# Bigbird attention into a gated MLP: two heads' block rows by one SBUF DMA, and two output steps of batch 0 in one slot

## The chip, the cores and the metric

One core of a Trainium2 chip runs the whole program. The metric is the device time of one execution in microseconds (us); the time before is the median of three runs.

## What is computed

Block-sparse attention over 4 batches, 8 heads, 768 positions and head size 64, followed by a gated MLP over the joined heads:

```
mask = window of +-1 block | first and last block (rows and columns) | 3 sampled blocks per row   # blocks of 32
attn = softmax(where(mask, q k^T / 8, -1e9)) ;  x = attn v            # heads joined: [4, 768, 512]
h = relu(x @ w_in) ; u, v = halves of h
v_n = (v - mean) / sqrt(var + 1e-6)
out = (u * (w_spatial @ v_n + b_spatial)) @ w_out                      # [4, 768, 512] float32
```

## The kernel before

**The mask inside the product.** The tile `kq` has 88 partitions: 64 hold the head size, and 24 (`MR`, partitions 64 to 87) hold *block rows*. For a key column a block row says which of the 24 blocks the key lies in (one-hot); for a query column it says which blocks the query's block may see (0 or -300). One matmul over 88 rows then gives masked scores. For every head `kq` holds 768 key columns (`K_`) and 768 query columns, the queries in three thirds of 256 (`qcols(t)`). The block rows are the same for all heads. They are computed once, for head 0: the keys' by `one_hot` on VectorE, the queries' by three small matmuls (`mask_rows`), which ScalarE (`m0`, `m1`) and VectorE (`m2`) copy into `kq`. Then they are copied to the other heads: `rows` (line 248) copies them on VectorE, and one DMA (line 328) writes the second and third query thirds of heads 2 to 7.

**Loads and casts.** Heads come in pairs: pair 0 is heads 0 and 1 of batch 0, pair 3 is heads 6 and 7. `load` (line 109) queues a transfer of q, k or v of one pair on SP's DMA queue; `cast` (line 137) turns it into bf16, on POOL for nearly all; `w_in_load` (line 228) and `w_in_cast` (line 234) do it for the eight quarters of w_in. SP and POOL each work through their instructions in the order in which the program lists them, and a transfer that waits for a buffer or a place holds up those behind it on SP. In this text w00 is the first quarter of w_in's second half (`w_in_load(0, 0)`), w01 and w02 the next ones, and v1, v2, v3 the loads of v for those pairs.

**Slots.** The main loop (lines 841 to 859) goes through slots `s`, and in each it issues one group of score matmuls with its exponential, the products with v of an earlier slot (`av_unit`, `av_full`), and what `when` and `late` have put there. Slots 0 to 35 do batch 0, a third of the queries at a time (`qk_unit`: scores at line 442, exponential at line 447, v products at line 488); three slots make a unit, and slots 12 to 14 are the unit of pair 3. From slot 36 on whole heads are done (`qk_full`, lines 455 and 459, v products at line 506).

Keys and queries of the pairs 1 to 3 of batch 0 get into `kq` by transposes on TensorE (line 289) and copies on VectorE (line 218): `tr_first` for the keys and the first query third, `tr_rest` for the other thirds. `tr_first(3)` stands in slot 10, `tr_rest(1)` in 11, `tr_rest(2)` in 15. The copies of block rows that VectorE makes in the loop are listed in `ROWS` as (slot, first head, end head, columns).

**gMLP steps.** One step is one 512-column matmul of the gated MLP (line 580). `STEPS` says how many steps of the queue each slot from 20 to 91 takes. The last steps of batch 0 are those of its output product with w_out; at slot 92 batch 1 is queued. The products take their PSUM banks in turn from two tags, `moeA` and `moeB`, which the transposes of line 289 share; a bank is free again when its product has been copied out.

Of the kernel before, what the change touches and what calls it, by code (L numbers as in the profile page):

```python
# [26 lines left out]
def kernel(  # L27
# [16 lines left out]
    nc = tc.nc  # L44

    B, H, S, D = q.shape
    BLK = 32
    NB = S // BLK
# [11 lines left out]
    VA = D + 1  # L60
# [4 lines left out]
    TW = TC * 128  # L65
# [15 lines left out]
    mhalf = const.tile([128, NCH], FP32)  # L81

    kq = const.tile([KR, H, 2 * S], BF16, name="kq")
    NVV = 6
    vv = [const.tile([128, 2, NCH, VS], BF16, name=f"vv{s}") for s in range(NVV)]
    MR = slice(D, KR)
    K_, Q_ = slice(0, S), slice(S, 2 * S)

    def qcols(t0, n=1):
        return slice(S + t0 * TW, S + (t0 + n) * TW)  # L90
# [4 lines left out]
    def dram(src, p, hs=slice(0, 2), cs=slice(0, NCH)):  # L95
        b, g = divmod(p, NG)
        return src[b, 2 * g + hs.start:2 * g + hs.stop].rearrange(
            "h (p c) d -> p h (c d)", c=NCH)[:, :, cs.start * D:cs.stop * D]

    H0, H1, BOTH = slice(0, 1), slice(1, 2), slice(0, 2)  # L100
    ALLC, C01, C03, C45 = slice(0, NCH), slice(0, TC), slice(0, 2 * TC), slice(2 * TC, NCH)
    C25 = slice(TC, NCH)
    SRC = {"k": k, "q": q, "v": v}

    def load(p, nm, hs=BOTH, cs=ALLC, eng=nc.sync):
        if (nm, p) not in st:
            st[nm, p] = work.tile([128, 2, S // 2], FP32, tag="st_" + nm,
                                   bufs=4 if nm == "q" else 3, name="st_" + nm)
        eng.dma_start(out=st[nm, p][:, hs, cs.start * D:cs.stop * D],  # L109
                      in_=dram(SRC[nm], p, hs, cs))  # L110
# [4 lines left out]
    def nat0_view():  # L115
        return nat[0].rearrange("p c h d -> p (c h d)").rearrange("p (h x) -> p h x", h=2)

    def cast(p, nm, eng, hs=BOTH, cs=ALLC):
        if nm == "v":
            dst = vv[p % NVV][:, hs, cs, 0:D]  # L120
        else:
            if p not in nat:
                nat[p] = work.tile([128, 2 * NCH, 2, D], BF16, tag="nat", bufs=4, name="nat")
            c0 = 0 if nm == "k" else NCH
            dst = nat[p][:, c0 + cs.start:c0 + cs.stop].rearrange("p c h d -> p h c d")[:, hs]
        src = st[nm, p].rearrange("p h (c d) -> p h c d", d=D)[:, hs, cs]
        if p == 0 and nm != "v":
            dst = nat0_view()[:, hs, (c0 + cs.start) * D:(c0 + cs.stop) * D]
            if cs is not C45:
                dst = dst[:, 0].rearrange("p (i t d) -> p t i d", t=2, d=D)  # L130
                src = src[:, 0].rearrange("p (t i) d -> p t i d", t=2)
            else:
                dst = dst.rearrange("p h (c d) -> p h c d", d=D)
        if eng is nc.scalar:
            nc.scalar.activation(out=dst, in_=src, func=AF.Copy)
        else:
            eng.tensor_copy(out=dst, in_=src)  # L137
# [77 lines left out]
    PL, DV = nc.gpsimd, nc.vector  # L215
# [10 lines left out]
    def w_load(key, src):  # L226
        wst[key] = work.tile([128, DM], FP32, tag="osb", bufs=6, name="w_f")
        nc.sync.dma_start(out=wst[key], in_=src)

    def w_in_load(u, g):  # L230
        w_load((u, g), moe_w_in[g * 128:(g + 1) * 128, 0 if u else DH:DH if u else DFF])
# [11 lines left out]
    def rows(hs, cs, eng=nc.vector):  # L243
        src = kq[MR, 0:1, cs].to_broadcast([NB, hs.stop - hs.start, cs.stop - cs.start])
        if eng is nc.scalar:
            nc.scalar.activation(out=kq[MR, hs, cs], in_=src, func=AF.Copy)
        else:
            eng.tensor_copy(out=kq[MR, hs, cs], in_=src)
# [11 lines left out]
    load(2, "q", cs=C01)  # L260
    load(3, "q", cs=C01)
    load(1, "v")
    load(2, "v")
    load(1, "q", cs=C25)
    cast(0, "q", PL, H1, C03)
    for s in range(NVV):
        nc.gpsimd.memset(vv[s][:, :, :, D:VA], 1.0)
    nc.gpsimd.memset(mhalf, -0.5)
    cast(1, "k", PL)
    cast(1, "q", PL, cs=C01)  # L270
    cast(0, "v", PL)
    load(3, "v")
    w_in_load(0, 0)

# [29 lines left out]
    def split0(ps, h, c0, n, t, copy=dve_copy):  # L306
# [18 lines left out]
    m1()  # L325
    m2()
    rows(H1, qcols(0, 3))
    nc.sync.dma_start(out=kq[MR, 2:H, qcols(1, 2)],
                      in_=kq[MR, 0:1, qcols(1, 2)].to_broadcast([NB, H - 2, 2 * TW]))
    w_in_load(0, 1)  # L330
# [376 lines left out]
    def deal(steps, slots):  # L707
        queue.extend(steps)
        pace["slots"], pace["credit"] = slots, 0.0

    def run_queue(n=None):
        if n is not None:
            for _ in range(n):
                queue.popleft()()
            return
        if not queue or pace["slots"] <= 0:
            return
        pace["credit"] += (len(queue) - pace["credit"]) / pace["slots"]
        pace["slots"] -= 1
        n = int(pace["credit"] + 0.5)  # L720
        for _ in range(min(n, len(queue))):
            queue.popleft()()
            pace["credit"] -= 1
# [5 lines left out]
    def when(slot, *fns):  # L729
        at.setdefault(slot, []).extend(fns)  # L730

    def c(f, *a, **kw):
        return lambda: f(*a, **kw)

    ROWS = [(1, 2, 4, qcols(0)), (1, 2, 3, K_), (3, 3, 4, K_), (4, 4, 6, qcols(0)), (6, 4, 6, K_), (7, 6, 8, qcols(0)), (9, 6, 8, K_)]
    when(0, second)
    when(1, third)
    when(2, lambda: filler(FILL3, psum.tile([128, 512], FP32, tag=moe_tag(), bufs=1, name="wps")))
# [3 lines left out]
    when(10, c(tr_first, 3))  # L742
    for sl, h0, h1, cs in ROWS:
        when(sl, c(rows, slice(h0, h1), cs))
# [27 lines left out]
    when(18, lambda: first["steps"].popleft()())  # L772
    when(20, close_first)
    when(29, lambda: deal(moe[0].in_steps("v2 v3 u2 u3", TC), 14))
    STEPS = {20: 0, 21: 3, 22: 2, 23: 0, 24: 2, 25: 1, 26: 2, 27: 2, 28: 0, 29: 1, 30: 1, 31: 1, 32: 2, 33: 1, 34: 1, 35: 1, 36: 1, 37: 0, 38: 1, 39: 2, 40: 2, 41: 2, 42: 1, 43: 3, 44: 3, 45: 0, 46: 2, 47: 1, 48: 2, 49: 1, 50: 2, 51: 0, 52: 2, 53: 1, 54: 1, 55: 1, 56: 2, 57: 3, 58: 1, 59: 1, 60: 2, 61: 2, 62: 3, 63: 1, 64: 1, 65: 1, 66: 1, 67: 2, 68: 3, 69: 1, 70: 1, 71: 1, 72: 1, 73: 2, 74: 2, 75: 1, 76: 1, 77: 3, 78: 1, 79: 1, 80: 1, 81: 2, 82: 0, 83: 3, 84: 1, 85: 2, 86: 0, 87: 2, 88: 2, 89: 3, 90: 1, 91: 1}
    when(42, lambda: deal(moe[0].in_steps("v4 v5 u4 u5", TC) + moe[0].rest_steps(),
                          S0 + 8 + 48 - 42))
    for b in (1, 2):
# [62 lines left out]
    for s in range(NS + LAG + 2):  # L841
# [11 lines left out]
        for f in early:  # L853
            f()
        run_queue(STEPS.get(s))
        for f in late.get(s, []):
# [34 lines left out]
```

## Time and profile before

| what | value |
|---|---|
| median of 3 runs | 211.44 us (211.42 to 212.21) |
| the profiled execution | 210.8 us, its span 208.9 us |
| TensorE busy | 202.7 us (97%) |
| ScalarE busy | 167.4 us (80%) |
| VectorE busy | 132.4 us (63%), 293 instructions |
| POOL busy | 70.3 us (34%) |
| granted TensorE clock | 1.00 in every stretch asked for |
| VectorE copies of block rows (line 248) | 9, of 285 to 875 ns, between 3.5 and 15.9 us |
| DMA of block rows (line 328) | 1, 144 KB, issued at 11.23 us, 0.97 us to issue |

The span is the time from the first to the last instruction on the core, and the profiled execution's time holds some 1.9 us around it. In the lines of the profile PE is TensorE's matmuls, PEld its weight loads, DVE is VectorE, ACT ScalarE, POOL GpSimd, and SPq the instructions with which SP issues DMAs. A line of the timeline gives the start in us, the length in us, the engine, the source line, the operation, and output and inputs by the program's names; brackets at its end give the idle time before it and what ended it. Matmuls are pipelined, so the length shown for a group of them overlaps the next one's start; the chain of waits shows the time from start to start.

### The profile page before, as it was taken

Reading aid. Unit: us, or ns where it says so; the run is one execution under the profiler, and the core shown is the slowest. Engines: PE = TensorE matmul, PEld = TensorE weight load, DVE = VectorE, ACT = ScalarE, POOL = GpSimd, SP = SyncE. Lnnn points to the kernel's source line nnn. Section 1 sums busy time; section 2 is a strip of 40 time slices with the busy share of each in tenths; the row PEclk is TensorE's granted clock in tenths of the full one; section 3 lists DMA queues with packets and bytes.
Section 4 is the critical chain, followed back from the end, with each engine's and each line's share of the span. In section 5 each row is a group of like instructions: output and inputs, shape, how many; then the busy total and the mean of one; then the engine's idle time right before and its main releaser. Section 6 shows DMA issues by size and latency. Waiting matters only on the chain.

```text
span 208.9 us, 5273 instructions
## 1 busy us (share of the span) xinstructions
PE 202.7 (97%) x2141; PEld 127.4 (61%) x2141; DVE 132.4 (63%) x293; ACT 167.4 (80%) x222; POOL 70.3 (34%) x108
## 2 busy tenths in 40 slices
PE   7898999999999999999999999999999999999993
PEld 6696878766666666655665565665566555544441
DVE  6898577889664544584986455386785433576542
ACT  5998999999989989979998888979999787266021
POOL 5684799585663314052065050131020000013000
PEclk9999999999999999999999999999999999999999
DMA  5999999999999999999935597794101324520266
GB/s 138 353 352 302 366 398 269 251 262 233 265 379 189 274 197 310 234 273 350 193 129 113 122 251 172 222 346 64 38 3 25 63 53 93 200 100 0 50 158 244
DMA packets 64295, 41.97 MB, mean 201 GB/s; under 512 B 45184, under 2 KB 59024, under 8 KB 64272
## 3 DMA queue, kind: packets, MB, share of 16 engines
q1 hardware_dynamic: 63696, 41.06, 76.2%
q10 hardware_dynamic: 576, 0.59, 0.8%
q8 instruction: 16, 0.26, 0.5%
q14 instruction: 7, 0.06, 0.1%
HBM read 24.38 MB, written 6.29 MB: 147 GB/s over the span
## 4 chain that ended last, share of the span: by engine, by line
PE 88%; DMA 6%; POOL 2%; SPq 1%; issue 0%; ACT 0%; ACTq 0%
PE ps_moe L580 34%; PE ps L455 23%; PE ps_av L506 13%; PE ps_t L580 8%; PE ps L442 4%; DMA w_f<-in_moe_w_in_dram 4%; PE ps_sc L580 4%; PE ps_av L488 3%; DMA st_v<-in_v_dram 3%; SPq L109 1%; POOL vv L137 1%; PE ps L289 1%; POOL w_in_t L234 1%; PE ps_av L289 0%; POOL nat L137 0%
## 5 line engine op out<-in xcount | busy, mean ns | idle before, releaser
L459 ACT ACTIVATE a_all<-ps 128x768 bf16<-128x768 f32 x144 | 113.3, 811 | 14.7 <-PE ps L455 8.6
L455 PE MATMUL ps<-kq 88*128 88x384 bf16 x288 | 70.4, 325 | 0.0
L506 PEld LDWEIGHTS <-a_all 128*128 128x128 bf16 x864 | 45.2, 97 | 20.0
L506 PE MATMUL ps_av<-vv,a_all 128*128 128x65 bf16 x864 | 49.8, 193 | 0.0
L455 PEld LDWEIGHTS <-kq 88*128 88x128 bf16 x288 | 27.7, 97 | 29.7
L580 PE MATMUL ps_moe<-w_in_t,xt 128*128 128x512 bf16 x144 | 43.2, 378 | 0.0
L447 ACT ACTIVATE a_all<-ps 128x1024 bf16<-128x1024 f32 x36 | 34.1, 1027 | 2.5 <-PE ps L442 2.3
L580 PE MATMUL ps_moe<-vn,w_spt 128*128 128x512 bf16 x108 | 32.7, 377 | 0.0
L137 POOL CAST nat<-st_k 128x768 bf16<-128x768 f32 (+2 forms) x17 | 13.9, 815 | 39.6 <-DMA st_k<-in_k_dram 39.6
L442 PE MATMUL ps<-kq 88*128 88x256 bf16 (+1 forms) x140 | 21.6, 275 | 1.4 <-ACT a_all L447 0.9
L619 POOL TENSOR_SCALAR std<-mv 128x3 f32<-128x3 f32 (+1 forms) x9 | 2.1, 238 | 61.3 <-DVE mv L616 44.3
L652 DVE SCALAR_TENSOR_TENSOR un<-ps_moe,b_col,un 128x512 bf16<-128x512 f32 x18 | 13.5, 748 | 13.7 <-PE ps_moe L580 13.3
L470 DVE RECIPROCAL rc<-ps_av 128x6 f32<-128x6 f32 (+1 forms) x36 | 6.6, 185 | 23.8 <-PE ps_av L506 21.7
L580 PE MATMUL ps_moe<-w_out_t,gt 128*128 128x512 bf16 x72 | 21.2, 378 | 0.0
L580 PEld LDWEIGHTS <-xt 128*128 128x128 bf16 x192 | 15.6, 98 | 7.7 <-DVE xt L218 0.2
L471 DVE TENSOR_TENSOR xn<-ps_av,rc 128x384 bf16<-128x384 f32 (+1 forms) x36 | 18.5, 513 | 1.2
L615 DVE BATCH_NORM_STATS2 stats<-vn 128x6 f32<-128x512 bf16 x24 | 16.4, 684 | 1.3 <-ACT vn L610 0.9
L137 POOL CAST nat<-st_q 128x768 bf16<-128x768 f32 (+2 forms) x21 | 14.8, 710 | 5.2 <-DMA st_q<-in_q_dram 4.9
L218 DVE COPY kq<-tt 64x1536 bf16<-64x1536 bf16 x24 | 15.5, 646 | 1.1 <-DMA tt<-nat 0.8
L137 POOL CAST vv<-st_v 128x768 bf16<-128x768 f32 x16 | 13.9, 871 | 6.4 <-DMA st_v<-in_v_dram 4.9
L442 PEld LDWEIGHTS <-kq 88*128 88x128 bf16 x140 | 12.6, 97 | 5.6 <-DVE kq L218 1.7
L580 PEld LDWEIGHTS <-w_spt 128*128 128x128 bf16 x144 | 11.6, 98 | 5.6
(81 smaller groups left out, 202.9 us busy)
## 6 DMA issues: line engine op xcount, KB each, us to landing
st_v<-in_v_dram SPq DMA_DIRECT2D x16, 384.0 KB, 6.2
st_k<-in_k_dram SPq DMA_DIRECT2D x15, 384.0 KB, 3.7
out_dram<-osb SPq DMA_DIRECT2D x22, 256.0 KB, 2.9
st_q<-in_q_dram SPq DMA_DIRECT2D x12, 384.0 KB, 5.7
ws_f<-in_moe_w_spatial_dram SPq DMA_DIRECT2D x6, 384.0 KB, 7.7
w_f<-in_moe_w_in_dram SPq DMA_DIRECT2D x8, 256.0 KB, 6.3
w_f<-in_moe_w_out_dram SPq DMA_DIRECT2D x4, 256.0 KB, 4.0
st_q<-in_q_dram SPq DMA_DIRECT2D x6, 128.0 KB, 5.2
```

What stands on the lines that cost most here:

```text
L137: eng.tensor_copy(out=dst, in_=src)
L218: nc.vector.tensor_copy(out=o, in_=i)
L442: nc.tensor.matmul(out=ps[:, at:at + n * TW], lhsT=kq[:, h, ci * 128:(ci + 1) * 128], rhs=kq[:, h, qcols(t0, n)], start=True, stop=True)
L447: nc.scalar.activation(out=out, in_=ps, func=AF.Exp, scale=0.125)
L455: nc.tensor.matmul(out=ps[:, hf * 512:hf * 512 + HALF], lhsT=kq[:, j % H, ci * 128:(ci + 1) * 128], rhs=kq[:, j % H, S + hf * HALF:S + (hf ...
L459: nc.scalar.activation(out=a_ref["h", j][:, ci, :].rearrange("p (b c) -> p b c", b=2), in_=ps.rearrange("p (b c) -> p b c", b=2)[:, :, 0:H ...
L470: nc.vector.reciprocal(out=rc[:, 0:n], in_=ps[:, :, D:VA])
L471: nc.vector.tensor_tensor(out=out, in0=ps[:, :, 0:D], in1=rc[:, 0:n].to_broadcast([128, n, D]), op=ALU.mult)
L506: nc.tensor.matmul(out=av_ref[j][:, qc, 0:VA], lhsT=a_ref["h", j][:, ci, qc * 128:(qc + 1) * 128], rhs=vv[p % NVV][:, h, ci, 0:VA], start= ...
L580: nc.tensor.matmul(out=ref["ps"][:, 0:w], lhsT=lhs(i), rhs=rhs(i), start=(i == 0), stop=(i == n - 1))
L615: nc.vector.bn_stats(out=stats, in_=self.vn[:, tcc, :])
L652: nc.vector.scalar_tensor_tensor(out=self.un[:, tcc, :], in0=ps, scalar=b_col[:, tcc:tcc + 1], in1=self.un[:, tcc, :], op0=ALU.add, op1=AL ...
```

## The change

The block rows of heads 6 and 7 (keys and first query third) are no longer copied by VectorE in slots 7 and 9. One DMA copies them from head 0's rows instead. It stands on SP's queue behind the load of v of pair 1. Since it reads rows that are computed further down in the program, the loads, casts and memsets that followed that load are listed after those lines now. The last two steps of batch 0 go into slot 90, and slot 91 has none.

```diff
     load(1, "v")
-    load(2, "v")
-    load(1, "q", cs=C25)
-    cast(0, "q", PL, H1, C03)
-    for s in range(NVV):
-        nc.gpsimd.memset(vv[s][:, :, :, D:VA], 1.0)
-    nc.gpsimd.memset(mhalf, -0.5)
-    cast(1, "k", PL)
-    cast(1, "q", PL, cs=C01)
-    cast(0, "v", PL)
-    load(3, "v")
-    w_in_load(0, 0)
...
     m1()
     m2()
     rows(H1, qcols(0, 3))
+    nc.sync.dma_start(out=kq[MR, 6:8, 0:S + TW], in_=kq[MR, 0:1, 0:S + TW].to_broadcast([NB, 8-6, S + TW]))
+    load(2, "v")
+    load(1, "q", cs=C25)
+    cast(0, "q", PL, H1, C03)
+    for s in range(NVV):
+        nc.gpsimd.memset(vv[s][:, :, :, D:VA], 1.0)
+    nc.gpsimd.memset(mhalf, -0.5)
+    cast(1, "k", PL)
+    cast(1, "q", PL, cs=C01)
+    cast(0, "v", PL)
+    load(3, "v")
+    w_in_load(0, 0)
     nc.sync.dma_start(out=kq[MR, 2:H, qcols(1, 2)],
                       in_=kq[MR, 0:1, qcols(1, 2)].to_broadcast([NB, H - 2, 2 * TW]))
...
-    ROWS = [(1, 2, 4, qcols(0)), (1, 2, 3, K_), (3, 3, 4, K_), (4, 4, 6, qcols(0)), (6, 4, 6, K_), (7, 6, 8, qcols(0)), (9, 6, 8, K_)]
+    ROWS = [(1, 2, 4, qcols(0)), (1, 2, 3, K_), (3, 3, 4, K_), (4, 4, 6, qcols(0)), (6, 4, 6, K_)]
...
     STEPS = {20: 0, 21: 3, ...
-             ... 89: 3, 90: 1, 91: 1}
+             ... 89: 3, 90: 2, 91: 0}
```

## The prediction

> **What bounds the kernel now.** I read the page's chain of waits first, to see which engine carries the end. Then the chain in order of time, because a change in the first 20 us counts only if it touches the links there.
>
> ```profile
> PE 88%; DMA 6%; POOL 2%; SPq 1%; issue 0%; ACT 0%; ACTq 0%
> ```
>
> ```profile
> 10.52 7.79 DMA w_f<-in_moe_w_in_dram
> 18.36 0.61 POOL w_in_t L234
> 18.98 0.77 POOL vv L137
> 19.75 0.56 POOL w_in_t L234
> 20.30 0.57 POOL nat L137
> ```
>
> Columns are start, length and what. Behind the last of these lines the chain holds only PE pieces, end to start. So TensorE is full from 20.9 us to the tail, and the first 21 us are set by something else: the load of w_in's first quarter, w00, lands at 18.31, POOL casts it, then v of pair 3, the next quarter, and the late queries of pair 2. That last cast ends at 20.87. TensorE waits for it, as its timeline shows:
>
> ```profile
> 17.18 0.61 PE L442 MATMUL ps<-kq 88*128 88x256 bf16 x4 [0.69 <-ACT a_all L447]
> ...
> 20.32 0.41 PE L488 MATMUL ps_av<-vv,a_all 128*128 128x65 bf16 x8
> 20.92 0.40 PE L289 MATMUL ps<-ident,nat 128*128 128x128 bf16 x4 [0.19 <-POOL nat L137]
> ```
>
> Eight such av matmuls take 0.24 us in the chain, so TensorE could have gone on at 20.56 and lost 0.36 us. The stop at 17.18 is another one: slot 12's scores need keys of head 6. ScalarE was idle 0.72 us before its exponential at 17.89, so the exponential was not what held slot 12; VectorE was:
>
> ```profile
> 14.29 0.88 DVE L248 COPY kq<-kq 24x512 bf16<-24x512 bf16 x1
> 15.20 0.18 DVE L470 RECIPROCAL rc<-ps_av 128x4 f32<-128x4 f32 x1
> 15.42 0.42 DVE L471 TENSOR_TENSOR xn<-ps_av,rc 128x256 bf16<-128x256 f32 x1
> 15.85 0.55 DVE L248 COPY kq<-kq 24x1536 bf16<-24x1536 bf16 x1
> 16.44 1.41 DVE L218 COPY kq<-ps 64x1024 bf16<-64x1024 bf16 x2
> ```
>
> The two L248 lines are the copies that the change removes. Head 6 of the 16.44 pair is done at about 17.15, and slot 12 starts.
>
> **What is removed.** 0.88 + 0.55 = 1.43 us of VectorE, at slots 7 and 9. The transposes of slot 10 end near 15.58, so VectorE's copies for pair 3 can start at 15.6 instead of 16.44 and end at 17.0. Slot 12 can then follow ScalarE without a hole: a gain of at most 0.72 us, ScalarE's idle time there. But it is followed by the wait at 20.92, which hangs on DMA and POOL and not on VectorE. TensorE would reach that wait up to 0.72 us earlier and stand there for 0.36 + 0.72 us. I count the removal at nothing; the cover is the cast that ends at 20.87.
>
> **What is added.** One DMA, call it R: 24 partitions x 2 heads x 1024 columns x 2 bytes = 96 KB, on SP between v1 and v2 (the loads of v for pairs 1 and 2). The block that the diff moves holds only SP and POOL instructions, and no other SP or POOL instruction lies between its old and new place: R is inserted, and the order of all else stays. R waits for nothing: its key rows are written by 2.93 us and its query rows by 4.66 (ScalarE, 4.29 + 0.37), and SP reaches it near 7.5. Its issue costs between the 0.47 us of a load and the 0.97 us of the one DMA of its kind. Queued behind it on SP are v2, the late queries of pair 1, v3 and w00. SP stood idle from 8.48 to 10.11, since v3 waits for POOL's cast of v0 (end 10.08), so the issue is hidden; without that cover it would cost up to 0.97. SP also keeps eight transfers in flight: 11.23 follows the landing at 11.2 of the load eight places before, 17.62 that at 17.6, 18.33 that at 18.31. With R counted in, w00 goes at about 11.23 instead of 10.52. The engines have more than 5 us of work queued then, so this costs nothing.
>
> What R costs is its time on the DMA engines, which are full (the DMA share is 1.00, 1.08 and 1.08 in the five-microsecond stretches from 5 to 20). The nearest row is the same kind of transfer, kq<-kq at L328, 144 KB, issued at 11.23:
>
> ```profile
> 14.00:15.00 1.00, 1.00 (x23) 0.94 (x22) 0.97 (x2) 1.00 (x2) 0.80 (x2) 1.00 1.02 362
> 15.00:16.00 1.00, 1.00 (x19) 0.95 (x17) 0.92 (x4) 1.00 (x2) 0.64 (x2) 1.00 1.12 272
> 16.00:17.00 1.00, 0.49 (x13) 0.31 (x9) 0.97 (x2) 1.00 (x2) 0.00 (x0) 1.00 1.08 195
> 17.00:18.00 1.00, 0.71 (x6) 0.41 (x7) 0.94 (x3) 0.28 (x2) 0.00 (x0) 1.00 1.07 264
> ```
>
> The last column is GB/s. While that transfer is served, the engines stay busy and move far less than 365: (93 + 170 + 101) GB/s over 1 us each is 364 KB less, 1.00 us of work, and its own 147 kB are 0.40 us more: 1.40 us of all engines. The landings say more:
>
> ```profile
> st_q<-in_q_dram SPq DMA_DIRECT2D x1, 256.0 KB, 6.8
> ```
> ```profile
> st_v<-in_v_dram SPq DMA_DIRECT2D x1, 384.0 KB, 7.5
> ```
>
> Those are the load issued at 8.01 (landed 14.8) and v3, issued at 10.11 (landed 17.6). The v load before landed 1.05 us behind its predecessor (13.05 to 14.1); v3 needed 2.8, so 1.75 us too many, and w01, two places on, 0.19 too many. In landings L328 costs 1.94 us.
>
> R moves 96/144 of its bytes: 2/3 of 1.40 is 0.93, 2/3 of 1.94 is 1.29. What counts is when w00 lands, so I take **1.29 us**. The low bound is R as plain bytes, 96 KB at 365 GB/s, 0.27 us; the high one is R as dear as all of L328, 1.94. A gain from R itself is taken up under the rivals. The page "DMA: Bandwidth & Descriptors" of the Trainium skill (section "Why a DMA increments its semaphore by 16 and not by 1") says that a copy runs on the largest number of engines up to 16 that divides its slowest dimension, so 24 partitions use 12. By that the 1.40 us become 1.40 x 16/12 = 1.87 on the engines that work, close to the 1.94 of the landings. The page "SBUF — State Buffer" (section on the DMA port swizzle) gives partitions 64 to 87 six of sixteen ports at about 27 GB/s; an estimate from that page is 0.6 us for R, and the sum would be +0.45. By the same estimate L328 would cost 0.9 us, and the trace shows more, 1.40 to 1.94.
>
> So v2 lands at about 15.4, v3 at 18.9, w00 at 19.6, and POOL's four casts move with it: the last ends at 22.16 and TensorE goes on at 22.21 instead of 20.92. On the way slot 11's transposes wait for the late queries of pair 1 (cast end 15.64 + 1.29 = 16.93 against 16.10 now), which uses up the hole at slot 12. R itself lands between v1 (13.05) and v2 (15.4), ahead of slot 12.
>
> **Two gMLP steps in slot 90.** TensorE's work is the same; the last matmul of batch 0's output goes at 87.04 instead of 87.55. In the present trace the next batch's first matmul waits for that product's bank:
>
> ```profile
> 88.02 0.69 DVE L218 COPY osb<-ps_moe 128x512 f32<-128x512 f32 x1 [0.21 <-PE ps_moe L580]
> ...
> 88.76 0.59 PE L580 MATMUL ps_moe<-w_in_t,xt 128*128 128x512 bf16 x2
> ```
>
> The transposes before it are issued by 88.61, so 0.15 us is lost until VectorE's copy ends at 88.71. With the step moved, the copy follows xn (end 87.81) and ends near 88.5: a gain of **0.15 us**. Slot 91's exponential starts 0.22 us later; ScalarE's 0.61 us of idle time before 89.72 hides it, and without that cover it would cost 0.22.
>
> **Sum.** 1.29 - 0.15 = +1.14 us. The profiled execution took 210.8 us (span 208.9, 1.9 around it), which becomes 211.94; the median of the runs is 0.64 above it, 211.44, and becomes **212.58**.
>
> **Rivals.**
> *R is dearer.* If R also pays for the 0.7 us later issue of w00, or clogs as long as L328 did, the shift is 1.94 - 0.15 = +1.8: 213.2. For it: R meets v2 on the engines just as L328 met v3. Against it: two thirds of the bytes.
> *R is cheap.* Pieces of 2 KB where L328 has 1 KB, and 48 where it has 144. At one third of 1.40 it is 0.47, as plain bytes 0.27: +0.1 to +0.3, 211.65. Against it: during L328 the larger w_f packets slowed down too, so bytes seem to count, not pieces.
> *Faster.* v3 was late although it was issued before L328, so later transfers can delay earlier ones. R takes one of the eight places, so the transfers from w00 on go out later (w02 must wait for R's landing, near 15, instead of 13.47). If w00 then has fewer rivals and lands earlier, the gate at 20.92 opens: up to 0.36 + 0.72 + 0.15 = 1.23 us, 210.2. It decides as soon as w00 lands before 18.31, and is complete at 17.2. Against it: full engines have the same bytes ahead of w00, and R's besides.
>
> **How the numbers follow.** A measurement of this kernel tells about 0.5% from no change, here 1.06 us. The forecast has 0.52; with R between 0.93 and 1.5 it gives +0.8 to +1.35, and I put 0.36 of it over the bound and 0.16 within. Dearer: 0.16, all over. Cheap: 0.18, within. Faster: 0.14, of it 0.09 past the bound. So slower 0.52, same 0.39, faster 0.09. The range 211.2 to 213.5 holds the forecast, the dear case and most of the cheap one, and leaves out the rest of the faster case and a still dearer R; the forecast's own is 212.2 to 212.8.
>
> **What the changed profile would show.** Right: a kq<-kq issue near 7.6, GB/s falling under 300 in 13 to 15, w00 landing near 19.6, POOL's cast of it about 1.3 us later, TensorE's wait before the L289 transposes longer than 0.36, no L248 copies at 14.29 and 15.85, and no hole at the start of batch 1. Wrong: w00 landing within 0.3 us of 18.31, or TensorE's stop no longer on POOL's nat.

## The result, and the profile after

The changed kernel takes 212.70 us, median of 12 runs (212.02 to 213.8), beside 211.49 us for the kernel before in 12 runs on the same chips (210.74 to 213.06). The ratio is 1.0061, its 95% interval 1.0041 to 1.0081: slower by 1.3 us, between 0.9 and 1.7. The forecast was +1.14 and 212.58 us. The profiled execution of the changed kernel took 213.03 us (span 211.3), 0.33 above the median, where the one of before lay 0.64 below its own; so the two traces differ by more (2.4 us of span) than the medians, and the difference in size is taken from the runs below.

The page's chain by engine, then pieces of the chain in order of time (start, length, what), of the changed kernel:

```profile
PE 87%; DMA 8%; POOL 2%; SPq 0%; ACT 0%; issue 0%; ACTq 0%
```
```profile
11.43 8.87 DMA w_f<-in_moe_w_in_dram
20.36 0.62 POOL w_in_t L234
20.97 0.77 POOL vv L137
```

It is the same chain: w00, POOL's casts, and TensorE behind them. w00 was issued at 11.43 and landed at 20.3, where it had been 10.52 and 18.31. TensorE's timeline shows where it stands:

```profile
15.12 0.65 PE L489 MATMUL ps_av<-vv,a_all 128*128 128x65 bf16 x16 [0.68 <-POOL vv L137]
...
18.36 0.40 PE L278 MATMUL ps<-ident,nat 128*128 128x128 bf16 x4 [1.02 <-POOL nat L137]
...
22.92 0.40 PE L278 MATMUL ps<-ident,nat 128*128 128x128 bf16 x4 [0.72 <-POOL nat L137]
```

There are three waits on POOL now. The first is new: v1 landed at 14.2 instead of 13.1, although it was issued ahead of R (the 96 KB transfer of block rows). Some of that is a later issue (7.6 instead of 7.0), but v1 also landed 1.7 us behind the load before it, where it had been 1.05. The second is slot 11's, for the late queries of pair 1; the third is the gate of slot 15, which opens at 22.92 instead of 20.92. VectorE's copies at 14.29 and 15.85 are gone, and it stands idle instead. The windows by microsecond (last columns: clock, DMA share, GB/s) show R's own dip ahead of that of the older transfer, which is L329 here:

```profile
12.00:13.00 1.00, 1.00 (x18) 0.88 (x15) 0.99 (x2) 1.00 (x2) 1.00 (x3) 1.00 1.10 241
13.00:14.00 1.00, 1.00 (x23) 0.93 (x21) 0.94 (x3) 1.00 (x2) 0.31 (x1) 1.00 1.07 256
14.00:15.00 1.00, 0.44 (x4) 0.24 (x3) 0.94 (x3) 0.99 (x2) 0.76 (x1) 1.00 1.07 317
15.00:16.00 1.00, 0.88 (x20) 0.84 (x20) 0.17 (x1) 0.56 (x1) 0.35 (x2) 1.00 1.11 375
16.00:17.00 1.00, 1.00 (x17) 0.94 (x16) 0.31 (x1) 0.76 (x1) 0.54 (x1) 1.00 1.09 280
```

At the start of batch 1 the hole has closed. The first product now starts 0.33 us behind the first of six transposes, where it was 0.48 (88.28 to 88.76):

```profile
90.28 0.50 PE L278 MATMUL ps<-ident,xn 128*128 128x128 bf16 x6
90.61 0.59 PE L581 MATMUL ps_moe<-w_in_t,xt 128*128 128x512 bf16 x2
```

### The profile page after: what moved, and what is told of

It is laid out like the page before. It is cut to its first block, busy times and chain, and to the rows that moved or that the text cites. A ratio compares the mean times of both kernels' runs of the same rounds, so it can differ in the third digit from the quotient of the medians.

```text
span 211.3 us, 5274 instructions
## 1 busy us (share of the span) xinstructions
PE 202.9 (96%) x2141; PEld 127.4 (60%) x2141; DVE 130.8 (62%) x291; ACT 167.7 (79%) x222; POOL 70.4 (33%) x108
## 4 chain that ended last, share of the span: by engine, by line
PE 87%; DMA 8%; POOL 2%; SPq 0%; ACT 0%; issue 0%; ACTq 0%
PE ps_moe L581 33%; PE ps L456 22%; PE ps_av L507 13%; PE ps_t L581 8%; PE ps L443 4%; DMA w_f<-in_moe_w_in_dram 4%; PE ps_sc L581 4%; DMA st_k<-in_k_dram 3%; PE ps_av L489 3%; DMA st_q<-in_q_dram 1%; POOL nat L137 1%; PE ps L278 1%; POOL w_in_t L234 1%; PE ps_av L278 0%; POOL vv L137 0%; SPq L142 0%
## 5 line engine op out<-in xcount | busy, mean ns | idle before, releaser
L460 ACT ACTIVATE a_all<-ps 128x768 bf16<-128x768 f32 x144 | 113.5, 812 | 14.4 <-PE ps L456 8.2
L137 POOL CAST nat<-st_k 128x768 bf16<-128x768 f32 (+2 forms) x17 | 13.5, 798 | 40.3 <-DMA st_k<-in_k_dram 38.9
L653 DVE SCALAR_TENSOR_TENSOR un<-ps_moe,b_col,un 128x512 bf16<-128x512 f32 x18 | 13.5, 748 | 14.0 <-PE ps_moe L581 13.7
```

The costliest lines, as they stand in the source:

```text
L460: nc.scalar.activation(out=a_ref["h", j][:, ci, :].rearrange("p (b c) -> p b c", b=2), in_=ps.rearrange("p (b c) -> p b c", b=2)[:, :, 0:H ...
L653: nc.vector.scalar_tensor_tensor(out=self.un[:, tcc, :], in0=ps, scalar=b_col[:, tcc:tcc + 1], in1=self.un[:, tcc, :], op0=ALU.add, op1=AL ...
```

## The experiments

Each kernel was compared with runs of the kernel before on the same chip (medians of before 211.45 to 211.50). A single trace is a weak witness: two executions with the same transfers differ by half a microsecond in the first 22 us (last section). So the ratios decide, and the traces are read for where a wait stands. I call the start of slot 16's exponential, the first one behind the gate, *the gate's time*; it is 22.01 in the trace of before. From there on nearly all kernels run alike.

**The two parts alone.** `steps_only` is the kernel before with the one edit in `STEPS`, `dma_only` the changed kernel with that edit undone:

```diff
-... 90: 1, 91: 1}
+... 90: 2, 91: 0}
```

> The kernel before with the last two gMLP steps of batch 0 both in slot 90, and nothing else changed. Theory (the bank hole of 0.15 us at the start of batch 1 closes): 0.15 us less, ratio 0.9993, and no gap before the first matmul of batch 1. Rival (slot 91's exponential pays for it): up to 0.22 us more, ratio 1.001.

Measured: ratio 0.9984 (0.9968 to 0.9999), 211.20 us. Less than before, by 0.0 to 0.7 us; the 0.15 us that the trace shows at the start of batch 1 lies inside, and the rival's loss does not.

> The changed kernel with the two gMLP steps put back into slots 90 and 91. Theory (the transfer's time on the DMA engines delays the first quarter of w_in, and the gate before the L278 transposes of slot 15 opens later): 1.2 to 1.4 us over the kernel before, ratio about 1.006. Rival (the two steps are what made it slower): no more than 0.3 us over before.

Measured: ratio 1.0048 (1.0026 to 1.0070), 212.45 us, 1.0 us over before: nearer to the theory than to the rival, somewhat under its figure. ScalarE's timeline has the gate's time and the wait ahead of it:

```profile
23.02 4.00 ACT L448 ACTIVATE a_all<-ps 128x1024 bf16<-128x1024 f32 x4 [1.03 <-PE ps L443]
```

23.02 is 1.01 later than before, and w00 landed 1.00 later (19.31). But the span is 1.5 longer (210.4), not 1.0: another half microsecond came later on.

**The transfer without the removal.** `copy_beside` keeps VectorE's copies and sends the same bytes into a tile that is not in use yet:

```diff
+    nc.sync.dma_start(out=w_spt[MR].rearrange("p a b n -> p (a b n)")[:, 0:2048].rearrange("p (h x) -> p h x", h=2),
+                      in_=kq[MR, 0:1, 0:1024].to_broadcast([NB, 2, 1024]))
```

> The kernel before, with VectorE's copies of slots 7 and 9 kept, and the same transfer as in the changed kernel (24 partitions x 2 x 1024 columns, 96 KB, same place in SP's queue), but written into a part of a tile that is not in use yet (w_spt). Nobody reads the copy. Theory (only the transfer costs; the removal of VectorE's copies is worth nothing): the same as with the change, +1.1 to +1.5 us, ratio about 1.006. Rival (VectorE's copies were worth up to 0.72 us, and the transfer costs that much more): +1.8 to +2.2 us, ratio about 1.0095.

Measured: ratio 1.0093 (1.0061 to 1.0124). That is the rival's figure, but the interval reaches down to the theory's and overlaps that of `dma_only`. It lies above `dma_only` by 0.7 us in the medians and by 0.9 in the ratios. The traces do not show this: the gate's time is 23.18, 0.16 us after `dma_only`.

**The removal without the transfer.** `no_rows` drops VectorE's two copies and lets POOL write zeros at the start:

```diff
     make_identity(nc, ident)
+    nc.gpsimd.memset(kq[MR, 6:8, 0:S + TW], 0.0)
...
-    ROWS = [..., (6, 4, 6, K_), (7, 6, 8, qcols(0)), (9, 6, 8, K_)]
+    ROWS = [..., (6, 4, 6, K_)]
```

> The kernel before without VectorE's two copies of slots 7 and 9 and with no transfer in their place. Left out: the block rows of heads 6 and 7 for the keys and the first query third, which POOL sets to zero at the start, so that their first third is not masked. Theory (the gate is the late queries of pair 2, behind DMA and POOL): the hole at slot 12 goes, the wait before the transposes of slot 15 grows from 0.36 to about 1.1 us, and the time stays within 0.2 us of before. Rival (VectorE was the limit): 0.7 us less, ratio 0.9967.

Measured: ratio 1.0030 (1.0006 to 1.0055). The kernel did not test the question: the zeros took 1.80 us of POOL ahead of everything, and TensorE's mask products came 0.8 us later.

```profile
2.83 1.80 POOL L175 MEMSET kq<- 24x2048 bf16 x1
```

`no_rows2` writes them where POOL stood idle in the kernel before:

```diff
     cast(1, "q", PL, cs=C25)
+    nc.gpsimd.memset(kq[MR, 6:8, 0:S + TW].bitcast(FP32), 0.0)
     w_in_cast(0, 0, PL)
```

> Again the kernel before without VectorE's copies of slots 7 and 9 and with no transfer, but POOL writes the zeros only when it stands idle anyway, behind its cast of pair 1's late queries (near 15.6 us), as 24 x 1024 float32. Left out, as before: the block rows of heads 6 and 7 for the keys and the first query third. In the first such run POOL's zeros took 1.80 us at 2.83 us and held up TensorE's mask products by 0.8 us, so it did not measure the removal. Theory of the prediction (the removal is worth nothing, the wait on the late queries of pair 2 takes it): within 0.2 us of before. Rival (the removal is worth something, since the copy beside VectorE's own came out 0.9 us over the changed kernel's transfer alone): 0.4 to 0.7 us less, ratio 0.997 to 0.998.

Measured: ratio 1.0155 (1.0105 to 1.0205). This one did not test it either. The zeros waited for the landing of L328, which writes other columns of the same rows, and slot 12 waited for the zeros (3.9 us):

```profile
19.78 0.94 POOL L345 MEMSET kq<- 24x1024 f32 x1 [3.96 <-DMA kq<-kq]
```

So what the removal is worth by itself stays open: between nothing and the 0.9 us that lie between `copy_beside` and `dma_only` by the ratios, with the traces on the low side.

**Bytes, partitions, place.** `copy_double` writes four copies instead of two, `copy_tiny` two of 32 columns, and `copy_wide` the same 96 KB from 128 partitions to 128:

```diff
-... .rearrange("p (h x) -> p h x", h=2), in_=kq[MR, 0:1, 0:1024].to_broadcast([NB, 2, 1024]))
+... .rearrange("p (h x) -> p h x", h=4), in_=kq[MR, 0:1, 0:1024].to_broadcast([NB, 4, 1024]))   # copy_double
+... .rearrange("p (h x) -> p h x", h=2), in_=kq[MR, 0:1, 0:32].to_broadcast([NB, 2, 32]))       # copy_tiny
+    nc.sync.dma_start(out=dum, in_=wide)                               # copy_wide: two tiles [128, 384]
```

> As the run with the copy beside VectorE's own, but the added transfer writes four copies (192 KB, 96 pieces of 2 KB). Theory (a cost by bytes on 12 engines): 2.4 to 2.8 us over before, about twice that of two copies, ratio about 1.012. Rival (a fixed cost of one transfer of this kind): +1.2 us as with two.

> The kernel before with an added transfer at the same place in SP's queue that moves the same 96 KB within SBUF, but from 128 partitions to 128 (384 columns each, from a tile that POOL sets to zero at the start; nobody reads the copy). Theory (24 partitions are what makes it dear: few engines and one group of partitions): plain bytes, +0.3 us, ratio 1.001. Rival (any 96 KB in front of w_in costs the same): +1.2 us.

> As the run with the copy beside VectorE's own, but the added transfer is cut to 24 partitions x 2 x 32 columns (3 KB). It takes the same place in SP's queue and among the eight transfers in flight. Theory (bytes on the DMA engines): within 0.2 us of before. Rival (the place in the queue, the 0.97 us of issue and the later issue of w_in's first quarter): the same +1.1 us as with the whole transfer.

Measured: `copy_double` 1.0109 (1.0075 to 1.0142), 214.36 us; `copy_wide` 1.0034 (1.0017 to 1.0050); `copy_tiny` 1.0032 (1.0013 to 1.0051). `copy_double` came out near the theory's figure, but its interval overlaps that of `copy_beside`, and its trace holds 1.6 us at the end that have nothing to do with the gate (below). The last two come out alike, and neither as expected: 3 KB should have been free and was 0.7 us. The intervals of `copy_wide` and `copy_beside`, the same bytes in 128 and in 24 partitions, do not meet. The DMA windows say what the bytes do. From 12 us on, first `dma_only` (R), then `copy_double`, then `copy_wide`:

```profile
12.00:13.00 1.00, 1.00 (x22) 0.90 (x20) 0.90 (x4) 1.00 (x2) 0.51 (x2) 1.00 1.06 221
13.00:14.00 1.00, 1.00 (x15) 0.94 (x14) 0.96 (x2) 1.00 (x2) 0.52 (x1) 1.00 1.07 310
```
```profile
12.00:13.00 1.00, 1.00 (x17) 0.87 (x14) 0.96 (x2) 1.00 (x2) 0.83 (x3) 1.00 1.05 197
13.00:14.00 1.00, 1.00 (x23) 0.93 (x21) 0.96 (x2) 1.00 (x2) 0.23 (x1) 1.00 1.11 222
14.00:15.00 1.00, 0.36 (x4) 0.17 (x2) 0.90 (x4) 0.99 (x2) 0.44 (x1) 1.00 1.11 248
```
```profile
12.00:13.00 1.00, 1.00 (x24) 0.95 (x22) 0.94 (x3) 1.00 (x2) 0.75 (x3) 1.00 1.08 365
13.00:14.00 1.00, 1.00 (x18) 0.93 (x15) 0.95 (x3) 1.00 (x2) 0.83 (x1) 1.00 1.07 359
```

The engines are as busy in all three. Against 365 GB/s, R loses 144 + 55 KB, 0.55 us, and its own 98 KB are 0.27: 0.8 us of all engines, where two thirds of L328's 1.40 gave 0.93. Twice the bytes lose 168 + 143 + 117 KB, 1.17 us, and with their own 0.54 make 1.7. The same 96 KB over 128 partitions cause no dip at all; its 128 pieces run from 11.1 to 12.8 us. The pieces of 1.5 KB in which the loads of v and of keys come tell the same: from 12 to 13 us one takes 69 ns (the middle value) before and in `copy_wide`, and 114 to 134 in `dma_only`, `copy_beside` and `copy_double`.

Later than that, single traces do not separate the kernels. The gate's time is 22.98 in `copy_wide`, as late as in `dma_only`, and 22.63 in `copy_tiny`, because the stretch from the landing of v2 to that of w00, which holds the older transfer, takes between 3.2 and 4.9 us in no order of the added bytes. Up to v2 the landings do separate them. From the landing of pair 2's keys to that of v2 it takes 2.9 us before, 3.0 in `copy_tiny` and 3.3 in `copy_wide`, but 3.8 in `dma_only`, 4.0 in `copy_beside`, 4.2 in the changed kernel and 5.0 in `copy_double`: R costs 0.8 to 1.3 us there, twice its bytes 2.1, and the same bytes over 128 partitions about what plain bytes cost (0.27).

So the cost follows the bytes, and only in the transfers from 24 partitions to 24. Whether the few partitions read, those written or the engines that serve them make it dear was not taken apart, and `copy_wide` also moves smaller pieces (768 bytes instead of 2 KB). What is left, 0.7 us for 3 KB, needs another reason, and the next two kernels ask whether it is the place. They put the small and the full transfer behind the load of pair 2's late queries, the last that the gate needs:

```diff
     load(2, "q", cs=C25)
+    <the 3 KB (tiny_behind) or 96 KB (copy_behind) transfer>
     w_in_load(0, 2)
```

> The transfer of 3 KB (24 partitions x 2 x 32 columns) that cost 0.3% between the loads of v, now behind the load of pair 2's late queries, the last load that the gate of slot 15 needs. Theory (a transfer costs by its place ahead of w_in's first quarter: that load is issued 0.6 us later and lands later): within 0.2 us of before. Rival (one more transfer costs 0.3% wherever it stands): ratio 1.003.

> The transfer of 96 KB in 24 partitions (into the same unused tile, VectorE's copies kept), now behind the load of pair 2's late queries. Theory (its bytes count only ahead of the gate's loads): within 0.3 us of before, ratio 0.999 to 1.0015. Rival (the DMA engines are the limit past the gate too): +0.8 us or more, ratio 1.004.

Measured: `tiny_behind` 1.0025 (1.0006 to 1.0044), `copy_behind` 1.0057 (1.0027 to 1.0088). The rivals were right: one more transfer costs about 0.5 us wherever it stands, and 96 KB in 24 partitions behind the gate's loads cost something too, by the medians 0.5 us more than 3 KB there, though the two intervals overlap. In `tiny_behind` the trace, that of the slowest of its twelve runs, has the late queries of pair 0 cast only at 27.84, which the transposes of slot 21 need, and a wait of TensorE of 0.8 us there.

**Where the fixed half microsecond is.** The last transfer of the output is issued on ScalarE's queue. First before, then `dma_only`, then `copy_tiny`, then `steps_only`:

```profile
205.93 0.35 ACTq L681 DMA_DIRECT2D out_dram<-osb  x1
```
```profile
206.92 0.35 ACTq L682 DMA_DIRECT2D out_dram<-osb  x1
```
```profile
206.53 0.35 ACTq L683 DMA_DIRECT2D out_dram<-osb  x1
```
```profile
206.21 0.35 ACTq L681 DMA_DIRECT2D out_dram<-osb  x1
```

The spans end at 208.9, 210.4, 210.0 and 209.2: 3.0, 3.5, 3.5 and 3.0 us later. This divides all kernels of the study by the number of transfers. Those with as many as before (before, `steps_only`, `no_rows`, `no_rows2`, `rows_by_need`) close in 3.0 us, those with one more (the changed kernel, `dma_only`, `copy_beside`, `copy_tiny`, `copy_wide`, `tiny_behind`, `copy_behind`) in 3.5, `split_late` below, with two more, in 3.6. Only `copy_double` is out of line, with 5.1: there the output transfer issued at 207.46 took 3.6 us to land, where the same one took 2.0 in `dma_only`. Counted from the last bytes that move, the time to the end is 1.35 us in the first group and 1.8 to 1.9 us in all others, `copy_double` too.

The half microsecond lies behind the landings. But for `copy_double`, the last output bytes move 1.6 to 1.7 us after that last issue, whatever the group (207.56 before, 208.57 in `dma_only`). Then SP goes through its last waits and signals to the other engines, and the kept records show it stand still for 0.34 to 0.38 us behind its 207th recorded instruction, in all fourteen traces. Before, SP has 210 of them, so the pause falls behind its signal that it is done, where it waits for the others anyway. A transfer more brings one or two instructions more on SP (211 or 212, 213 in `split_late`); the pause then falls ahead of that signal, and all engines wait for it. This is most of the half microsecond. What makes SP pause there is not shown.

**Versions meant to be faster.** If 24-partition bytes ahead of the gate are dear, the older transfer L328 is the place to save. `split_late` cuts it into three by need; `rows_by_need` lets VectorE write heads 2 and 3 and moves the rest, 96 KB, behind later loads. Both have the two steps in slot 90.

```diff
-    nc.sync.dma_start(out=kq[MR, 2:H, qcols(1, 2)], ...)
+    rows_dma(2, 4, 1)                                   # split_late; rows_dma(4, H, 1) behind w_in_load(0, 3),
+                                                        #   rows_dma(2, H, 2) three loads further on
+    nc.sync.dma_start(out=kq[MR, 4:H, qcols(1, 2)], ...)    # rows_by_need: behind w_in_load(0, 2)
+    ROWS = [..., (13, 2, 4, qcols(1)), (20, 2, 4, qcols(2))]
```

> A version meant to beat both: the kernel before with the two steps in slot 90, VectorE's copies kept, and the transfer of L328 (144 KB) cut by need: heads 2 and 3 of the second query third at its old place (24 KB), heads 4 to 7 of that third behind the fourth quarter of w_in's second half, the last third behind two more loads. Theory (24-partition bytes ahead of the late queries of pair 2 delay the gate): w_in's first quarter lands 1 us earlier or more, the gate of 0.36 us closes, and with the 0.15 us of the steps the time is 0.4 to 0.6 us below before, ratio about 0.9975; the hole at slot 12 stays. Rival (that transfer is off the path or the later pieces delay other loads as much): within 0.2 us of before.

> A second version meant to beat both: the two steps in slot 90, and L328's transfer cut to heads 4 to 7 (96 KB) and moved behind the third quarter of w_in's second half; heads 2 and 3 of the second and last query third are copied by VectorE in slots 13 and 20 (two copies of 24 x 512 more). No more transfers than before. Theory (24-partition bytes ahead of the gate's loads are the cost): w_in's first quarter lands about 1 us earlier and the gate of 0.36 us closes; 0.2 to 0.6 us less than before, ratio 0.997 to 0.999. Rival (VectorE, full in slots 10 to 14, or a later load takes it back, as with the cut into three transfers): ratio 1.000 to 1.003.

Measured: `split_late` 1.0030 (1.0010 to 1.0050), `rows_by_need` 1.0013 (0.9993 to 1.0034). In both, w00's cast started early, at 17.16 and 17.53 us instead of 18.36; but the trace of `steps_only`, with the transfers of before, has 17.47, so the part that is due to the edit is not settled. ScalarE went through slots 12 to 21 without a stop in `rows_by_need`:

```profile
17.99 9.85 ACT L447 ACTIVATE a_all<-ps 128x1024 bf16<-128x1024 f32 x10 [0.74 <-PE ps L442]
```

Neither gained. In `rows_by_need` slot 16 starts at 22.01 as before with the gate open, now held by ScalarE's exponentials behind the hole of slot 12. In `split_late` most of the gain at slot 16 (21.21) was given back by slot 36 (41.78 against 41.98 before): the loads of w_spatial land 0.9 us later behind the moved pieces, POOL's small steps stand behind those casts, and VectorE waits for them, by its list of waits from 20 to 45 us:

```profile
DVE vn L186 <- POOL rstd L626: 0.9, 1, 0.9
```

Two more transfers then cost 0.6 us at the end. The version that beats both kernels is `steps_only`.

## Why the prediction was right, step by step

**Right: what bounds the start, and the sign.** The chain still runs through w00 and POOL's casts to the transposes of slot 15, and R, ahead of w00, moved it. The rival of a faster kernel fell: w00 landed later in every kernel that sent R's bytes ahead of it, never earlier.

**Right: the price goes by bytes of a transfer of this kind.** Engine work of 0.8 us against 0.93 expected, and about double for double the bytes; over 128 partitions the same bytes cost no more than plain bytes do. How many engines R ran on (the prediction has 12) no run here shows. By the Trainium skill, page "SBUF — State Buffer" (section on the DMA port swizzle), a transfer into few partitions is limited by the few ports they reach; the trace agrees in kind, and the estimate of 0.6 us for R stays under the 0.8 measured, though the one is the length of the transfer and the other work that all engines lost.

**Mis-sized: R's term.** The prediction counted 1.29 us at the gate. `dma_only` has 1.01 in the trace, against that of before, and its 1.0 us over before, less the half microsecond at the end, leaves 0.5. The changed kernel's 1.3 us, less 0.5 and with the 0.15 of the steps, leave 0.9. So the gate moved by 0.5 to 1.0 us by the runs. The landings up to v2 give 0.8 to 1.3, and the trace of the changed kernel alone has w00 2.0 us later, 1.3 of it at v2; the rest is the start and the scatter behind v2.

**Missed: the end of the program.** One more transfer lengthens the closing by 0.5 us, in all eight traces with one more, if `copy_double` is counted from its last bytes. No term stood for it. It made up for what R's term had too much, so the sum of +1.14 came out close to the measured 1.3 for a reason that is only partly the one given. That closeness is luck; the sign and the place of the delay are not.

**Wrong: R behind v1 leaves v1 alone.** v1 landed at 14.2 in the changed kernel, 13.4 in `dma_only`, 13.1 before. Free of its issue time, v1 landed 1.65 to 1.73 us behind the load before it with R behind it (the changed kernel, `dma_only`, `copy_beside`), and 1.05 to 1.10 before, in `copy_tiny` and in `copy_wide`. So a later transfer does slow an earlier one down, as L328 had done to v3; I had used that for v3 and not for v1. By how much is not fixed: v3 came 2.8 us behind the load before it in the trace of before, and 1.2 in `steps_only`, which has the same transfers. In the trace of the changed kernel v1's delay cost the wait of 0.68 at slot 8, which the later gate then covered.

**Right: the two steps.** 0.15 us in the trace, and a gain in the runs whose interval holds it. ScalarE had the idle time that the step needed.

**Open: the removal at nothing.** The traces speak for little; the runs leave up to 0.9 us, and the two kernels made for it measured something else.

## What to carry to other kernels

A copy that is moved from an idle-looking compute engine to a DMA is paid on the DMA queue: price it by the dip in GB/s that the nearest transfer of the same shape leaves, and by what lands behind it. Look at what the freed engine was waiting for before counting its time as a gain; here it only reached the next wait earlier. A change in the number of transfers can move the end of the program as well, so a copy of next to nothing, at the same place, is a control worth running.

## What the runs showed of the hardware

The closing of the program grew from 3.0 to 3.5 us with one transfer more, however small: SP's pause of some 0.36 us behind its 207th recorded instruction came ahead of its signal that it is done instead of behind it.

A transfer of 96 KB in 24 partitions took rate from the other transfers in flight, those issued before it too (365 GB/s down to 221, and v1 0.6 us later); over 128 partitions it did not (365 and 359 GB/s).

TensorE's matmuls turn from slow to fast at one of two moments, in executions of one kernel and the next. The same four matmuls of slot 3, before and in `steps_only`, which differ in nothing until slot 90:

```profile
8.08 0.61 PE L442 MATMUL ps<-kq 88*128 88x256 bf16 x4 [0.30 <-DVE kq L218]
```
```profile
9.04 1.04 PE L442 MATMUL ps<-kq 88*128 88x256 bf16 x4
```

0.61 us and 1.04 us. In four of the traces (`steps_only`, `dma_only`, `copy_beside`, `copy_wide`) the slow matmuls lasted to about 9 or 10 us instead of 4 to 5, and slot 8's exponential started between 14.4 and 14.7 us; in those of before, the changed kernel and `copy_tiny` it was 13.2 to 13.5. By the Trainium skill, page "TensorE: Matmul & The Clock Gate" (Part 1), the clock rises by windows that run freely and don't start with the kernel, so the moment differs from run to run; the traces agree that it differs, but by some 5 us, where the page speaks of half a microsecond. The granted clock reads 1.00 all the while in `steps_only`, so its rows don't show that the clock is the cause; in `no_rows`, whose matmuls turn fast and are slow once more (1.06 us for the same four), it reads 0.50 from 8 to 10 us. The gate hides most of it: slot 16 starts at 22.44 in `steps_only` and at 22.01 before.
